# Three-stage Fourier and MLP kernel on one core: the odd outputs' two products of the second batch made one piece, and another order of the operations

## The chip, the core and the metric

The kernel runs on one core of one Trainium2 chip. The metric is the device time of one execution in microseconds (us). A core has engines that run side by side: TensorE (PE: matrix products; its weight loads are PEld), VectorE (DVE), ScalarE (ACT), GpSimd (POOL) and SyncE (SP), which here issues the transfers. Each engine works through its own instructions in the order in which the program gives them to it, and waits where an instruction needs what another engine, or a transfer, has not yet delivered.

## The reference

The input x has two batches of 3008 tokens with 256 values each. A Fourier transform along the tokens and one along the values are taken and the real part kept; the 6016 tokens that result go through two MLPs.

```python
X = np.fft.fft(x, axis=1)                    # x: (2, 3008, 256)
X = np.fft.fft(X, axis=2)
t = X.real.astype(np.float32).reshape(6016, 256)
h = t @ moe_w_in                             # (256, 2048)
r = np.maximum(h, 0.0)
t = (r * r) @ moe_w_out                      # (2048, 256)
h = t @ moe2_w_in
return (h * (1.0 / (1.0 + np.exp(-1.702 * h)))) @ moe2_w_out
```

## The kernel before

**Numbers in two halves.** The MLPs multiply in a rounded float32 format. So that the result keeps its precision, each operand is split into a rounded high part and a low part that holds the rest, and a product is made of three: high by high, high by low, low by high. The high part is a cast (on ScalarE, L1087), the low part a subtraction (`sub`, L182: `gl`, `eo`, `w`), which runs on VectorE or GpSimd. The weights come as pairs of 32-bit words and are put together by a run of small elementwise operations on ScalarE and VectorE (L294 to L324), named after the weight piece: `i0` to `i3` and `u0` to `u3` for the first MLP's two weights, `j` and `v` for those of the second.

**Stage 1** (until about 441 us) is everything up to the end of the first MLP. x is folded by symmetries (operations `f0` to `f5`, TensorE at L557 and L568; sums on VectorE at L489 to L520; copies out of PSUM on ScalarE at L281 and L595). Then the transform along the tokens is done as products with cosines and sines: for each batch b even outputs in two pieces (`e{b}0`, `e{b}1`, L693) and the odd outputs (`o{b}`). For the odd ones there are two products, `o{b}E0` (with `zc`) and `o{b}E1` (with `zs`), each of 16 matmuls at L652 into two PSUM banks; `o{b}c0`, `c1` copy one bank to SBUF, `o{b}s0`, `s1` (VectorE, L757 and L758) add and subtract the other, and the operations on `o{b}2` and `o{b}3` split the results, the last ones (`N`, at L768 in one case) making the value-axis part that only TensorE can turn around.

The 16 matmuls are emitted by `halves()` (L644). It multiplies parts with all 128 rows and parts with 64 rows, and its argument `turned` says which come first; by default the 64-row parts are last. The row count matters to the trace below: a product of 128 rows and one of 64 rows follow each other less tightly than two of the same kind.

**The first MLP** lies in the same stage, in 96 steps: six blocks of 512 tokens (one of 480, one of 484) by 16 slices of 128 hidden values, in the order `TURNS`. Step n has these operations:

- `Fn`: six matmuls (L791 to L793, three each for two banks, `psa`): the slice of h.
- `Pn`: VectorE adds a term of one row to the first bank (L1070), and the second bank to that and from that (L1072, L1073), which are the two halves of h. After L1070 the first bank is free, after L1073 the second.
- `Rn`: relu and square, on ScalarE in two halves (L1081, L1082) or on VectorE (L1079).
- `Hn` and `Gn`: the high part on ScalarE (L1087), the low part on GpSimd or VectorE (L182, `gl`).
- `Bn`: twelve matmuls with w_out (L806) into `psb`: eight of `gh` and four of `gl`.

**Stage 2** (441 to 937 us) is the second MLP, six blocks of eight units, TensorE at L1126 and L1147.

**What sets the order.** A string `ORDER` names every operation of stage 1 once, and the program emits them in that order; so it fixes each engine's queue. `HOME` names the engine of an operation where it isn't the usual one (A ScalarE, G GpSimd, V VectorE). `RINGS` says for six kinds of buffer which of them each use takes: `a0` and `a1` are the PSUM banks (two each) that `Fn`, the odd products and `o13N` write, `gh`, `gl`, `h` and `p` are buffers of the steps. All transfers go through SyncE's queue, in the order of the operations ending in `D`.

Of the kernel before, what the change touches and what calls it, by code (L numbers as in the profile page):

```python
# [40 lines left out]
f0D f0Db dfD f0a0 f0s0 f0p f0a1 df f0s1 f0m f1D f0mb f0pb f1s0 i0D f1a0 nD i0A f0E f1m f0Eb f1p i0L f2D ny f1u u0D nm
f0O f0Ob f0e1 c00D f1E nA f2s0 f1O nL f0e0 u0A f1e0 f2a0 f2m f2p c01D f2u f2E f1o c02D nC se i0C u0C f2O i0O f2e1 f0o
f2e0 i0S e00N nO i0P u0L i1D i0N f1e1 nS e00n f2o i0M u0S e00E u0O e00m e00c i0H e01E e01c e00s e01s i1L e01N c03D e00h
f0g f1g u0P e01n e00l i1O f2g e01h i1A i0l o0E0 o0c0 e01hb e01m i1C e01l
F0 nP i1S
F1 u0H P0 R0 o0s0 o0E1 H0 e01lb P1 u0l i1P o0c1 o0s1 G0 R1 o02h o02l o02hb f3D
F2 o02lb
F3 P2 B0 i1M o02N u1D P3
F4 H1 G1 o02n P4
F5 R2 R3 H2  # L50
F6 B1 i1N i1H R4 H3 u1L P5 u1A
F7 G2 i1l H4 B2 G3 G4 R5 P6 u1O H5
F8 P7 P8 u1C G5 B3 o03hb R6
F9 i2D i2A i2C u1S R7 X3.1 u1P i2S H6 G6 X3.0
F10 B4 H7 u1H u2D i2L B5 u1l P9 P10 R8 B6 G7 H8 i2O
F11 P11 R9
F12 G8 B7 u2L H9 R10 i3D i2P R11 H10 P12 G9 H11 u2O i2M B8 i2N i2H u2A
F13 G10 R12 G11 B9
F14 P13 u2C B10 i2l H12 G12 R13 P14
F15 i3A P15 B11 H13 G13 X11.0 X11.1  # L60
F16 i3C R14 B12 i3L H14
F17 R15 u2S H15 P16 P17
F18 u2P R16 G14 B13 o03h u2H R17 P18 i3S i3O
F19 H16 P19
F20 i3P G15 u2l B14 H17 G16 P20 R18 G17 H18 u3D i3N i3M u3L B15 R19 B16 H19 u3A
F21 G18 R20 H20
F22 u3O B17 P21 c10D P22 i3H G19 B18 G20 Y19 i3l
F23 R21 B19 H21 R22
F24 P23 G21 R23 H22 X19.0 X19.1 P24 R24 u3C
F25 H23 P25 R25 B20 o03l f3s0 H24 o03lb u3S  # L70
F26 G22 P26 B21 u3P G23
F27
F28 P27 R26 j0D B22 u3H B23
F29 P28 G24 o03N P29 R27 u3l f3a0 H25 f3m H26 H27 f4D G25 B24
F30 o03n G26 R28
F31 G27 f3p H28 f3v P30 R29 B25 Y27 G28 B26 B27 f4s0 f4a0 H29 P31 G29
F32 R30 H30 X27.0 X27.1 R31
F33 B28 c11D f3u P32 G30 P33
F34 H31 B29 f3w P34 R32 f4p f3E H32 f3O f3e0 R33 B30 G31 Y31 f4m
F35 B31 R34 f4u H33 G32 f3o P35  # L80
F36 G33 f5D H34 f3e1
F37 G34 X31.0 X31.1 R35 B32 P36 f5a0
F38 f5s0 f5m f4v R36 B33 P37 H35 P38
F39 f5p G35 B34 f4w H36
F40 P39 R37 f4O f5u P40 B35 G36 R38 v0D
F41 H37 f4o f4E R39 B36 H38 f5v P41 f4e0 f5w f4e1
F42 G37 R40 G38 f5E P42 f5e1 B37 f5e0 f5O H39 f5o =x e10E H40 e10n e10m G39 e10c
F43 e10s R41 e10h
F44 f5g B38 H41 R42 P43 H42 P44 e10l G40
F45 B39 P45 e11E e11n R43 G41 e11c e11m R44 R45 G42 e11s  # L90
F46 e11h c12D e11hb B40 e11l H43
F47 j0L P46 B41
F48 P47 H44 e11lb G43 f4g
F49 P48 c13D j0A j0C B42 R46 H45 j0S f3g B43
F50 j0O G44 H46 P49 R47 G45 R48
F51 P50 G46 B44 B45 H47
F52 B46 H48 R49 G47 R50 P51 G48 j0P B47 P52 H49 G49 H50 X47.0
F53
F54 X47.1 j01 B48 R51 P53 R52 H51 G50 P54 G51 j02 R53
F55 P55 H52 B49 G52 j03  # L100
F56
F57 P56 P57 R54 B50 j04 H53
F58 B51 j0H1 H54 G53 j0H0
# [1 line left out]
F60 B53 o1c1 o1s1 o12h j1D o12hb o12lb G56 o12l B54 o12N P60 o12n H57 H58 o13h
F61 R59 B55 G57 H59
F62 B56 P61 o13l G58 v0A R60 P62
F63
F64 G59 R61 H60 v0L =c B57 P63 R62 G60
F65 H61 R63 P64 v0O R64 P65 B58 v0C B59 v0S B60 R65  # L110
F66 v0P H62 G61 v1D P66 v0H H63
F67 G62 v0l P67 H64 o13N j1A B61 H65 tk o13n R66 R67 G63 G64
F68 B62
F69 G65 P68 P69 H66 R68 j1C R69 B63
F70 G66 X63.0 X63.1
F71 j1S j1L B64 H67 H68 B65 P70 R70 P71 G67 H69
# [18 lines left out]
F90 P89 H85 G85 H86 B84 G86 yaH
F91 ybH0 P90 R88 R89 H87 R90 ybl0 H88 P91 B85 B86 R91
F92 G87 P92 G88
F93 H89 R92 yal P93 H90
F94 y2 B87 B88 H91 G89 y3 G90 G91 R93
F95 ybH1 P94 B89 B90 P95 H92 G92 ybl1 H93 R94 B91 G93 H94 R95 G94 H95 B92 G95  # L140
# [1242 lines left out]
```

## Time and profile before

| | |
|---|---|
| median of 3 runs | 939.01 us (938.97 to 939.48) |
| the profiled execution | 939.21 us, span of its instructions 937.0 us |
| granted TensorE clock | 1.00 of full speed in every stretch (the 2.4 GHz level) |
| TensorE busy | 930.3 us of the span (99%) |
| busy until 40 us, 40 to 441 us, 441 to 937 us | 38.00, 400.44, 491.83 us |

The span runs from the first to the last instruction on the core; the execution's own time is 2.2 us longer. In a row of the timeline stand the start, the time from the start of the first to the end of the last of the x instructions put together, the engine, the line, the operation, what it writes and reads, and in square brackets how long the engine sat idle before it and what ended that. Matmuls are pipelined: one begins before the last has ended, so the distance from start to start is what one costs TensorE.

### The profile page before, as it was taken

Reading aid. Unit: us, or ns where it says so; the run is one execution under the profiler, and the core shown is the slowest. Engines: PE = TensorE matmul, PEld = TensorE weight load, DVE = VectorE, ACT = ScalarE, POOL = GpSimd, SP = SyncE. Lnnn points to the kernel's source line nnn. Section 1 sums busy time; section 2 is a strip of 40 time slices with the busy share of each in tenths; the row PEclk is TensorE's granted clock in tenths of the full one; section 3 lists DMA queues with packets and bytes.
Section 4 is the critical chain, followed back from the end, with each engine's and each line's share of the span. In section 5 each row is a group of like instructions: output and inputs, shape, how many; then the busy total and the mean of one; then the engine's idle time right before and its main releaser. Section 6 shows DMA issues by size and latency. Waiting matters only on the chain.

```text
span 937.0 us, 10882 instructions
## 1 busy us (share of the span) xinstructions
PE 930.3 (99%) x4274; PEld 777.5 (83%) x4274; DVE 693.1 (74%) x807; ACT 574.8 (61%) x620; POOL 252.6 (27%) x139
## 2 busy tenths in 40 slices
PE   9999999999999999999999999999999999999998
PEld 9688888888878788888888888888888888888886
DVE  7999999988976889978888665665675576466453
ACT  4798987557667775686766544544454455455443
POOL 0668486602333646353123200020030011000000
PEclk9999999999999999999999999999999999999999
DMA  8521333600200120200320100110010011000001
GB/s 316 200 74 62 116 135 127 239 3 24 68 21 0 45 91 1 75 16 7 126 91 1 59 29 1 45 46 1 1 66 22 1 43 46 0 1 39 7 1 43
DMA packets 12915, 53.53 MB, mean 57 GB/s; under 512 B 1344, under 2 KB 4544, under 8 KB 9664
## 3 DMA queue, kind: packets, MB, share of 16 engines
q1 hardware_dynamic: 12864, 52.84, 15.5%
q8 instruction: 33, 0.54, 0.2%
q14 instruction: 18, 0.15, 0.0%
HBM read 37.36 MB, written 15.48 MB: 56 GB/s over the span
## 4 chain that ended last, share of the span: by engine, by line
PE 91%; DVE 5%; ACT 2%; DMA 1%; issue 0%; SPq 0%; DVEq 0%; ACTq 0%
PE psb L1147 27%; PE psb L806 25%; PE psc L1126 22%; PE psa L791 4%; PE psa L792 4%; PE psa L793 4%; PE psa L652 1%; PE psb L652 1%; DMA xt<-in_x 1%; PE psa L568 1%; DVE gl L182 1%; PE psa L693 1%; DVE ue L312 0%; ACT zc L595 0%; DVE t L489 0%
## 5 line engine op out<-in xcount | busy, mean ns | idle before, releaser
L806 PE MATMUL psb<-gh,w 128*128 128x512 f32 (+2 forms) x768 | 215.3, 387 | 0.0
L182 POOL TENSOR_TENSOR gl<-h,gh 128x1024 fp32r<-128x1024 f32 (+2 forms) x56 | 141.3, 2532 | 134.6 <-PE psb L806 58.3
L806 PEld LDWEIGHTS psb<-gh,w 128*128 128x128 f32 x768 | 143.7, 188 | 27.8 <-ACT h L1082 0.5
L1147 PE MATMUL psb<-gh,w 128*128 128x512 f32 (+2 forms) x576 | 163.9, 386 | 0.0
L1218 DVE TENSOR_TENSOR g<-u,psc 128x1024 f32<-128x1024 f32 (+2 forms) x48 | 57.6, 1200 | 115.8 <-PE psc L1126 115.8
L1220 ACT ACTIVATE g<-g 128x1536 f32<-128x1536 f32 (+2 forms) x48 | 70.4, 1467 | 95.5 <-DVE g L1218 95.5
L1147 PEld LDWEIGHTS psb<-gh,w 128*128 128x128 f32 x576 | 108.1, 188 | 20.8
L1087 ACT CAST gh<-h 128x1024 fp32r<-128x1024 f32 (+2 forms) x96 | 97.8, 1029 | 38.6 <-PE psb L806 30.8
L806 PE MATMUL psb<-gl,w 128*128 128x512 f32 (+2 forms) x384 | 117.2, 386 | 0.0
L182 DVE TENSOR_TENSOR gl<-g,gh 128x2048 fp32r<-128x2048 f32 (+3 forms) x50 | 110.4, 2212 | 0.4 <-ACT gh L1195 0.4
L1081 ACT ACTIVATE h<-h 128x1024 f32<-128x1024 f32 (+2 forms) x79 | 81.8, 1036 | 18.1 <-DVE h L1073 18.1
L1195 ACT CAST gh<-g 128x2048 fp32r<-128x2048 f32 (+3 forms) x50 | 90.4, 1813 | 0.1
L911 POOL TENSOR_TENSOR ue<-raw 128x512 f32<-128x512 f32 (+2 forms) x12 | 22.1, 1863 | 249.7 <-DMA raw<-ydram 243.3
L1147 PE MATMUL psb<-gl,w 128*128 128x512 f32 (+2 forms) x288 | 87.9, 386 | 0.1
L1082 ACT ACTIVATE h<-h 128x1024 f32<-128x1024 f32 (+2 forms) x79 | 82.4, 1043 | 2.5
L806 PEld LDWEIGHTS psb<-gl,w 128*128 128x128 f32 x384 | 72.1, 188 | 14.0
L1070 DVE SCALAR_TENSOR_TENSOR p<-n,w1n_t,psa 128x512 f32<-128x512 f32 (+2 forms) x96 | 70.0, 729 | 12.0 <-PE psa L793 11.8
L1217 ACT ACTIVATE g<-psc 128x512 f32<-128x512 f32 (+2 forms) x48 | 28.4, 592 | 76.2 <-PE psc L1126 76.2
L791 PE MATMUL psa<-eo,w 128*128 128x512 f32 (+2 forms) x192 | 74.7, 389 | 0.0
L793 PE MATMUL psa<-eo,w 128*128 128x512 f32 (+2 forms) x192 | 74.1, 386 | 0.0
L792 PE MATMUL psa<-eo,w 128*128 128x512 f32 (+2 forms) x192 | 74.1, 386 | 0.0
L1072 DVE TENSOR_TENSOR h<-p,psa 128x512 f32<-128x512 f32 (+2 forms) x96 | 65.0, 677 | 12.2 <-DVE p L1070 1.0
(186 smaller groups left out, 1528.1 us busy)
## 6 DMA issues: line engine op xcount, KB each, us to landing
ydram<-o SPq DMA_DIRECT2D x14, 512.0 KB, 2.8
xt<-in_x SPq DMA_DIRECT2D x5, 1024.0 KB, 5.9
cst<-in_dfts SPq DMA_DIRECT2D x8, 576.0 KB, 7.3
raw<-in_w1i SPq DMA_DIRECT2D x4, 1024.0 KB, 5.6
raw<-in_w1o SPq DMA_DIRECT2D x4, 1024.0 KB, 7.8
raw<-in_w2i SPq DMA_DIRECT2D x4, 1024.0 KB, 5.2
raw<-in_w2o SPq DMA_DIRECT2D x4, 1024.0 KB, 4.9
raw<-ydram SPq DMA_DIRECT2D x4, 1024.0 KB, 4.7
```

What stands on the lines that cost most here:

```text
L182: eng.tensor_tensor(out=o, in0=a, in1=f32(b), op=ALU.subtract)
L791: T.matmul(o, lhsT=w[:, 0, fs], rhs=t[:, par, 0, 0:wd], start=True, stop=False)
L792: T.matmul(o, lhsT=w[:, 0, fs], rhs=t[:, par, 1, 0:wd], start=False, stop=False)
L793: T.matmul(o, lhsT=w[:, 1, fs], rhs=t[:, par, 0, 0:wd], start=False, stop=True)
L806: T.matmul(acc[j][ec][:, s, 0:wd], lhsT=w[:, hl, e0:e0 + P], rhs=(gh, gl)[gi][:, s, 0:wd], start=(first and hl == 0 and gi == 0), stop=(la ...
L1081: A.activation(out=hv, in_=hv, func=AF.Relu)
L1082: A.activation(out=hv, in_=hv, func=AF.Square)
L1087: A.copy(st["gh"][:, :, 0:wd], st["h"][:, :, 0:wd])
L1126: T.matmul(bank, lhsT=w[:, hl, slot * P:(slot + 1) * P], rhs=x[:, yl, 0:wd], start=(first and hl == 0 and yl == 0), stop=(hl == 1), skip_g ...
L1147: T.matmul(o[:, s, 0:wd] if j < BLKS - 1 or ec == 0 else o[s][:, 0:wd], lhsT=weights[1, 1, f // 4][:, hl, e0:e0 + P], rhs=g[:, 2 * i + s, ...
L1195: A.copy(gh[:, at], gs[u - 1][:, at])
L1220: A.activation(out=g[:, 1:4], in_=g[:, 1:4], func=AF.Gelu_apprx_sigmoid)
```

## The change

Three things change.

1. `halves` is called with `turned=True` for the second of the two odd products, in both batches: it takes its 64-row parts first.
2. In the second batch the two products `o1E0` and `o1E1` become one operation `o1E`, so that nothing can stand between their matmuls: the 64-row parts that end the first product are followed by the 64-row parts that begin the second. In the first batch they stay `o0E0` and `o0E1`.
3. `ORDER` is another one throughout stage 1, and `HOME` and three of the `RINGS` (`a0`, `a1`, `h`) go with it. In the first 96 steps VectorE has 29 of the low parts G where it had 40 (GpSimd 67 where it had 56), and 15 of the R where it had 17; six low parts of the second MLP's w_in move from GpSimd to VectorE (GpSimd 2 where it had 8).

Line numbers of the changed kernel are higher by 1 up to about L740 and by 7 behind it (the odd products at L653, `Fn` at L798 to L800, `Bn` at L813, `o13N` at L775).

```diff
--- before.py
+++ after.py
...
-F59 j0l0 P58 G54 R55 P59 R56 o1E0 j0l1 o1E1 H55 B52 o1c0 G55 R57 R58 H56 o1s0
...
+F59 B52 H55 P59 o1E j0l0 H56 R58 G55 o1c0 o1s0
...
-    "a0": "0101010101010101010101010101010101010101010101010101010101010101010101010101010101010101010101010101"
+    "a0": "0101010101010101010101010101010101010101010101010101010010101010101010101010101010110101010101010101"
-    "a1": "0100101010101010101010101010101010101010110101010101010101010101010101010101010101010101010101010101"
+    "a1": "0100101010101010101010101010101010101010101010101010101011010101010101010101010101010101010101010101"
...
@@ -738,14 +739,20 @@
             w = make().rearrange("p a b -> p (a b)")
             return w[:, 0:wd], *(w[:, i * wd:(i + 2) * wd].rearrange("p (r k) -> p r k", r=2) for i in (1, 3))
 
+        both = []
         for par in range(2):
-            @op(f"{name}E{par}")
-            def _(par=par):
+            def sums(par=par):
                 c0, c1 = cst[b, 2][:, :, 0:wd], cst[b, 3][:, :, 0:wd]
                 pe = held[par] = ps_b() if f"{name}E{par}" in IN_B else ps_a()
                 z = (zc[b], zs[b])[par]
                 halves(pe[:, 0, 0:wd], pe[:, 1, 0:wd],
-                       [(z[:, :, 2 + par, 0:P], c0), (z[:, :, 3 - par, 0:P], c1)])
+                       [(z[:, :, 2 + par, 0:P], c0), (z[:, :, 3 - par, 0:P], c1)], turned=par == 1)
+
+            if b:
+                both.append(sums)
+                ops[f"{name}E"] = lambda: [f() for f in both]
+            else:
+                ops[f"{name}E{par}"] = sums
 
             @op(f"{name}c{par}")
             def _(par=par):
```

The order itself is best seen on the engines. **TensorE at the odd products of the second batch** (about 270 to 283 us in the trace of before). Before, the operations are B51, F58, F59, o1E0, o1E1, B52, F60; the rows show the second half of that, from F59 on:

```order
L791 MATMUL psa<-eo,w 128x512
L792 MATMUL psa<-eo,w 128x512
L793 MATMUL psa<-eo,w 128x512
L652 MATMUL psa<-cst,zc 128x376 x8
L652 MATMUL psa<-cst,zs 128x376 x8
L806 MATMUL psb<-gh,w 128x512 x2
L806 MATMUL psb<-gl,w 128x512 x2
L806 MATMUL psb<-gh,w 128x512 x4
```

After, they are F59, B52, o1E, F60, B53:

```order
L813 MATMUL psb<-gh,w 128x512 x2
L813 MATMUL psb<-gl,w 128x512 x2
L813 MATMUL psb<-gh,w 128x512 x4
L813 MATMUL psb<-gl,w 128x512 x2
L813 MATMUL psb<-gh,w 128x512 x2
L653 MATMUL psa<-cst,zc 128x376 x8
L653 MATMUL psa<-cst,zs 128x376 x8
L798 MATMUL psa<-eo,w 128x512
L799 MATMUL psa<-eo,w 128x512
L800 MATMUL psa<-eo,w 128x512
```

B52 has moved from behind the two products to ahead of them, and what follows them now is F60, whose banks come from the same two rings as theirs. (The order counts eight matmuls for an odd product, the trace sixteen records.)

**TensorE at `o13N`** (about 316 us before; sel_t is the small matrix by which it multiplies). Before, F66 and F67 stand right ahead of it:

```order
L791 MATMUL psa<-eo,w 128x512
L792 MATMUL psa<-eo,w 128x512
L793 MATMUL psa<-eo,w 128x512
L768 MATMUL psa<-eo,sel_t 128x376 x2
L806 MATMUL psb<-gh,w 128x512 x2
L806 MATMUL psb<-gl,w 128x512 x2
```

After, F64, F65 and B57 do, and F66 comes behind it:

```order
L813 MATMUL psb<-gh,w 128x512 x4
L813 MATMUL psb<-gl,w 128x512 x2
L813 MATMUL psb<-gh,w 128x512 x2
L775 MATMUL psa<-eo,sel_t 128x376 x2
L798 MATMUL psa<-eo,w 128x512
L799 MATMUL psa<-eo,w 128x512
```

Between `o13N` and the last F there are now the twelve matmuls of a B.

**ScalarE in the first 22 us.** The two-row products of x leave PSUM through `zc` and `zs` (L595 and L281; L596 and L282 after), which the folds of the later parts wait for; L294 and L300 (L295 and L301 after) widen weights: ue<-raw is the piece `i0` the first time, `u0` the second time. Before:

```order
L294 ACTIVATE ue_132<-raw_128 128x1024
L300 ACTIVATE ue_132<-raw_128 128x1024
L440 ACTIVATE nyq_106<-nyq_106 128x24
L595 ACTIVATE zc_200<-psa_163,nyq_106 128x65 x4
L294 ACTIVATE w1n_t_105<-w1n_raw_101 128x16
L300 ACTIVATE w1n_t_105<-w1n_raw_101 128x16
L595 ACTIVATE zc_200<-psa_134,nyq_106 128x65 x4
L294 ACTIVATE ue_234<-raw_184 128x1024
L595 ACTIVATE zc_200<-psa_207,nyq_106 128x65 x4
L281 COPY zs_258<-psb_220 128x512
```

After:

```order
L301 ACTIVATE w1n_t_105<-w1n_raw_101 128x16
L441 ACTIVATE nyq_106<-nyq_106 128x24
L295 ACTIVATE w1n_t_105<-w1n_raw_101 128x16
L282 COPY zs_197<-psb_162 128x512
L295 ACTIVATE ue_216<-raw_190 128x1024
L301 ACTIVATE ue_216<-raw_190 128x1024
L596 ACTIVATE zc_222<-psa_126,nyq_106 128x65 x4
L301 ACTIVATE ue_227<-raw_193 128x1024
L596 ACTIVATE zc_222<-psa_155,nyq_106 128x65 x4
L596 ACTIVATE zc_222<-psa_234,nyq_106 128x65 x4
```

The widening of u0 stands between the first and the second copy of zc, where before the second copy of zc stood ahead of it and one more behind it.

## Rows read from the trace of the kernel before

**Rows 1.** The page: busy time of each engine over the span.
```profile
PE 930.3 (99%) x4274; PEld 777.5 (83%) x4274; DVE 693.1 (74%) x807; ACT 574.8 (61%) x620; POOL 252.6 (27%) x139
```

**Rows 2.** TensorE's waits: line waited at, releaser, us in total, times, longest.
```profile
PE psa L768 <- DVE p L1070: 0.6, 1, 0.6
PE psb L652 <- ACT ue L300: 0.5, 1, 0.5
```

**Rows 3.** Timeline of TensorE, even outputs and first odd product of batch 0.
```profile
24.16 0.49 PE L693 MATMUL psa<-cst,zc 64*128 64x189 f32 x4
24.48 0.49 PE L693 MATMUL psa<-cst,zs 64*128 64x189 f32 x4
24.89 0.91 PE L693 MATMUL psa<-cst,zc 128*128 128x189 f32 x4
25.64 1.19 PE L693 MATMUL psa<-cst,zs 128*128 128x189 f32 x4
26.66 0.80 PE L693 MATMUL psb<-cst,zc 128*128 128x188 f32 x4
27.30 0.80 PE L693 MATMUL psb<-cst,zs 128*128 128x188 f32 x4
28.03 0.59 PE L693 MATMUL psb<-cst,zc 64*128 64x188 f32 x4
28.45 0.48 PE L693 MATMUL psb<-cst,zs 64*128 64x188 f32 x4
30.59 4.23 PE L652 MATMUL psb<-cst,zc 128*128 128x376 f32 x16 [0.50 <-ACT ue L300]
```

**Rows 4.** Timeline of TensorE, the two odd products of batch 1.
```profile
272.35 4.15 PE L652 MATMUL psa<-cst,zc 128*128 128x376 f32 x16
276.43 4.26 PE L652 MATMUL psa<-cst,zs 128*128 128x376 f32 x16
280.62 0.73 PE L806 MATMUL psb<-gh,w 128*128 128x512 f32 x2
```

**Rows 5.** Timeline of TensorE, VectorE and GpSimd around the wait at L768.
```profile
316.16 0.39 PE L792 MATMUL psa<-eo,w 128*128 128x512 f32 x1
316.39 0.39 PE L793 MATMUL psa<-eo,w 128*128 128x512 f32 x1
317.33 0.61 PE L768 MATMUL psa<-eo,sel_t 128*128 128x376 f32 x2 [0.56 <-DVE p L1070]
...
311.46 2.89 DVE L312 TENSOR_SCALAR ue<-ue 128x1024 uint32<-128x1024 uint32 x1
...
316.54 0.73 DVE L1070 SCALAR_TENSOR_TENSOR p<-n,w1n_t,psa 128x512 f32<-128x512 f32 x1
...
311.40 2.40 POOL L182 TENSOR_TENSOR gl<-h,gh 128x1024 fp32r<-128x1024 f32 x1 [0.52 <-PE psb L806]
```

**Rows 6.** Timeline of ScalarE, 18 to 20 us.
```profile
18.62 1.16 ACT L294 ACTIVATE ue<-raw 128x1024 f32<-128x1024 f32 x1 [2.15 <-DMA raw<-in_w1o]
```

**Rows 7.** Instructions of L312 and L182: count, ns min/median/max, first and last start.
```profile
L312 DVE TENSOR_SCALAR ue<-ue x14: 678/690/2901, 21.6 to 476.5; 128x1024 uint32<-128x1024 uint32 x14
...
L182 POOL TENSOR_TENSOR gl<-h,gh x56: 2211/2414/3468, 41.4 to 433.1; 128x1024 fp32r<-128x1024 f32 x43, 128x968 fp32r<-128x968 f32 x8, 128x960 fp32r<-128x960 f32 x5
...
L182 DVE TENSOR_TENSOR gl<-h,gh x40: 1147/1213/2141, 68.5 to 440.9; 128x1024 fp32r<-128x1024 f32 x21, 128x960 fp32r<-128x960 f32 x11, 128x968 fp32r<-128x968 f32 x8
```

**Rows 8.** Timeline of VectorE, GpSimd and TensorE, first steps of the MLP.
```profile
37.96 0.54 DVE L757 TENSOR_TENSOR ue<-ue,psb 128x376 f32<-128x376 f32 x1
...
38.88 0.74 DVE L1070 SCALAR_TENSOR_TENSOR p<-n,w1n_t,psa 128x512 f32<-128x512 f32 x1
...
40.92 1.22 DVE L324 CUSTOM_DVE_ANT_0 ue<-ue 128x2048 uint16<-128x2048 uint16 x1
...
41.38 3.04 POOL L182 TENSOR_TENSOR gl<-h,gh 128x1024 fp32r<-128x1024 f32 x1 [2.07 <-ACT gh L1087]
...
45.02 0.61 PE L806 MATMUL psb<-gl,w 128*128 128x512 f32 x2
```

More of the change, by code (lines that the diff above doesn't have):

```diff
@@ L37 @@
 WARM = {0: 24, 2: 2}
-HOME = {**dict.fromkeys("""u0L j0L v0L v1L X3.1 X11.1 X63.1 X79.1""".split(), "A"), **dict.fromkeys("""f3s0 f4s0 f5s0 i0l u0l i3l u3l u1l e01l e01lb o02l o02lb i1M i3M o03l e10l e11l o12lb o12l o13l y0 y1 ybl1""".split(), "G"), **dict.fromkeys("""i1l o0c1 o02n R5 R7 G6 G10 i2l R13 G16 G17 G18 R20 G24 G26 G27 R33 G36 G37 G38 G39 G40 e11n G41 G43 G44 G45 G46 G47 R50 j01 R51 G52 R54 j04 G53 G54 o1c0 G56 o12n G57 G58 G60 R65 R68 R69 G69 G70 G71 j14 R74 R76 R77 G75 G76 R79 G78 G81 G83 G85 R90 G87 G90 G93 R95 G94 G95""".split(), "V")}
+HOME = {**dict.fromkeys("""u0L v0L v1L X3.1 X11.1 X63.1 X79.1""".split(), "A"), **dict.fromkeys("""f3s0 f4s0 f5s0 i0l u0l u3l u1l e01l e01lb o02lb o02l i1M i2M i3M o03l e10l e11l o12l o13l y0 y1 y3""".split(), "G"), **dict.fromkeys("""i3l i1l j0L o0c1 o02n R5 R7 G6 G10 G11 i3L G13 R19 G19 G20 G27 G28 G32 G37 G38 f5o G39 R43 R44 e11n e11c G42 R49 G47 G49 j0l0 G55 o1c1 R59 R61 G58 o12n o13n G61 G64 R67 G65 G66 j1L R68 G69 j13 R77 R78 G77 j1l1 j1l0 R83 G80 G81 R91 G92 G93 R95 G94 G95""".split(), "V")}
@@ L39 @@
 IN_B = ('f0O', 'f1O', 'f2O', 'e00N', 'e01E', 'e01N', 'o0E0', 'o0E1')
 ORDER = """
[L41 to L103, printed above, removed]
@@ L104 @@
-F59 j0l0 P58 G54 R55 P59 R56 o1E0 j0l1 o1E1 H55 B52 o1c0 G55 R57 R58 H56 o1s0
[L105 to L116, printed above, removed]
@@ L135 @@
[L135 to L140, printed above, removed]
+f0D f0Db f0a0 dfD f0s0 nD f0p f1D f0s1 f0a1 f0m df f0mb f0E f0pb f1a0 se f0O f1s0 f1p f1m f0Ob f2D ny f1u f2s0 nL i0D nm
+u0D nA f2a0 f0o f2m f2p f0Eb f1O i0A nC f2u i0C i0L f0e0 u0L nO f0e1 f1E f1e0 f2E i0O i0S f1o c02D i0P f2O f2e0 c01D
+c00D i1D u0O f2e1 f2o u0A e00N e00E i0M i0N nS f1e1 e01E u0C nP e00n e00c i0H u0S e00s i1L e01c c03D e00m f1g e00h e01s
@@ new lines @@
+i1A e00l f0g u0P e01N i0l e01n e01m i1C u1D e01hb o0E0 e01h i1O e01l o0c0 i1S
+F0 o0s0 P0 u0H
+F1 u0l f2g P1 o0E1 e01lb i1P o0c1
+F2 R0 o0s1
+F3 i2D H0 P2 R1 G0 o02hb o02h H1 B0 P3 R2 u1A o02lb o02l o02N i1N i1M o02n
+F4 P4 H2 i1H
+F5 R3 R4 H3 P5 G1 H4 G2 G3 B1
+F6 u1C
+F7 B2 R5 u1S i1l G4 P6 u1L
+F8 B3 u1O f3D P7 u2D H5 i2L i2A G5 X3.0 R6 P8 i2C
+F9 u1P
+F10 i2S X3.1 R7 P9 H6 u1H R8 B4 H7 G6 u2L H8 u1l P10 i2O c11D B5 R9
+F11 P11 R10 H9 G7 B6
+F12 B7 i2P c12D G8 P12 R11 H10 i3D H11 G9 i2M
+F13 P13 B8 G10 R12 i2N G11 u2A i2H i2l H12 B9
@@ new lines @@
+F14
+F15 B10 u2C G12 R13 i3A P14 B11 P15 o03h
+F16 u2O H13 X11.0
+F17 X11.1 u3D i3C R14 u2S i3L i3S G13 u2P H14 P16 B12 u2H B13
+F18 P17 i3O R15 H15 G14 R16
+F19 u2l P18 H16 G15 R17 P19 B14 H17
+F20 R18
+F21 G16 B15 R19 G17 P20 i3P i3M i3N P21 H18 R20
+F22 B16 H19 P22 o03hb G18 G19 H20 i3H i3l f3s0 B17 R21
+F23 R22 B18 G20 H21 Y19 P23 G21 B19 X19.0
+F24 H22 X19.1 P24
+F25 u3A u3L P25 B20
+F26 R23 f3a0 P26 o03l
+F27 B21 R24 H23 G22 u3C P27 H24 R25 o03lb u3O j0D u3S H25 G23 f3m G24 R26 u3P
+F28 B22 u3H P28 H26 B23 R27 u3l
@@ new lines @@
+F29
+F30 R28 f4D P29 B24 G25 G26 f3p H27
+F31 P30 H28 B25 G27 o03N B26 R29 H29 R30 f4a0 G28 B27 P31 f3v
+F32 o03n G29 H30 Y27 R31 H31 X27.0
+F33 G30 X27.1 B28 P32 P33 f4s0 f4m R32 R33 f4p
+F34 B29 P34 H32 G31 G32 f3u
+F35 R34 B30 f3w Y31 P35 H33 c10D f3O G33 f3o f3E f3e1 B31 f4v X31.0 R35 f3e0 X31.1
+F36 P36
+F37 H34 B32
+F38 P37 v0D G34 H35 f4u
+F39 P38 f4w B33
+F40 R36 G35 R37 P39 H36 P40 f5D G36 f4O
+F41 f5s0 B34 f4o P41 f5a0 f5p f5m R38
+F42 H37 f4E H38 B35 G37 P42 B36 f5u R39 f5v f5w R40 H39 f4e1 f4e0 f5O f5E f5e0 R41 G38 B37 f5e1 f5o e10E G39 e10n =x
@@ new lines @@
+e10m e10c
+F43 e10s
+F44 P43 B38 H40
+F45 B39 e10h P44 G40 f4g H41 c13D P45 R42 R43 R44 e11E e10l e11n G41 e11c H42 R45 G42 B40 f5g e11s H43 G43 e11h H44 e11m
+F46 P46 e11l e11hb
+F47 e11lb j0A R46 B41 P47 H45
+F48
+F49 G44 P48 B42 R47
+F50 R48 P49 H46 j0L B43 G45 P50
+F51 G46 j0C B44 H47
+F52 B45 P51 H48 R49 R50 H49 R51 G47 B46 P52 G48 B47
+F53 j0S G49 H50 X47.0 R52 j0O X47.1
+F54 j0P B48 G50 P53 H51
+F55 j1D j01 B49 j02 R53 H52 P54 P55
+F56 R54 G51 j03
+F57 G52 B50 j04 R55 f3g P56
+F58 H53 j0H1 P57 B51 G53 j0H0 R56 P58 R57 j0l1 H54 G54
@@ new lines @@
+F59 B52 H55 P59 o1E j0l0 H56 R58 G55 o1c0 o1s0
+F60 o1c1 o1s1 B53 G56
+F61 o12h o12hb R59 H57 P60 B54 o12lb P61 R60 G57 o12l
+F62 P62 B55 R61 H58 o12N o13h G58 o13l H59
+F63 B56 v0A P63 o12n v0L G59
+F64 H60
+F65 R62 R63 B57 P64 H61 v0O o13N G60 P65
+F66 B58 H62 B59 o13n
+F67 v0C G61 tk R64 v0S P66 B60 H63 B61
+F68 H64 R65 G62 v0P G63 P67 v0H
+F69 B62 G64 H65 R66 v0l H66 R67 P68 P69 G65 B63 G66 j1L v1D X63.0 j1A R68
+F70 X63.1 H67
+F71 j1C j1S P70 R69 B64
+F72 G67 B65 P71 P72 j1O j1P
+F73 H68 R70 R71 H69 =c R72
@@ new lines @@
+F74 G68 B66 P73 j11 G69 B67
+F75 H70 P74 H71
+F76 G70 B68 P75
+F77 B69 G71 P76 B70 R73 j12 H72 H73
+F78 G72 R74 j13 B71 G73 R75 H74 P77 R76 G74
+F79 R77 j14 P78 P79
+F80 H75 B72 G75 R78 H76 j1H1
+F81 B73 P80 yD G76 R79
+F82 H77 B74 R80 P81 H78 R81
+F83 G77 j1H0 B75 j1l1 P82 G78 B76
+F84 H79 G79 H80 P83 P84 j1l0 R82 B77 R83 v1A v1C G80 H81 B78 v1L G81 B79 X79.0
+F85 X79.1 v1S H82 R84 B80 G82 v1O P85
+F86 P86 H83 G83
+F87 P87 H84 R85 v1P B81
+F88 jlD R86 G84
+F89 B82 v1H P88 P89 H85
+F90 R87 G85 B83 v1l P90 H86
@@ L141 @@
+F91 R88 H87 B84 G86
+F92 G87 P91 P92
+F93 R89 y0 B85 y2 R90 B86 R91 H88
+F94 H89 H90 B87 G88 y1 G89 R92 ybH1 G90 P93 P94
+F95 B88 H91 y3 P95 yaH B89 ybl1 R93 G91 H92 R94 yal B90 H93 G92 G93 H94 R95 ybH0 B91 G94 H95 ybl0 B92 G95
 """
 RINGS = {
-    "a0": "0101010101010101010101010101010101010101010101010101010101010101010101010101010101010101010101010101"
+    "a0": "0101010101010101010101010101010101010101010101010101010010101010101010101010101010110101010101010101"
           "0101010101010101",
-    "a1": "0100101010101010101010101010101010101010110101010101010101010101010101010101010101010101010101010101"
+    "a1": "0100101010101010101010101010101010101010101010101010101011010101010101010101010101010101010101010101"
@@ L148 @@
     "gl": "012012012012012012012012012012012012012012012012012012012012012012012012012012012012012012012012",
-    "h": "0123402134021343042130421423014230123401234013420134201342013420134202013420134201342013134201342013"
-          "4201343420134201",
+    "h": "0123402134021341402314020231402314031240312402341024130241302413024131302413024130241302024130241302"
+          "4130202413024130",
     "p": "0101010101010101010101010101010101010101010101010101010101010101010101010101010101010101010101010101"
```

18 lines of the change are left out of this document (removed).

## The prediction, made before the changed kernel had run

> **What bounds the kernel now.** I read the page's busy times first: TensorE is busy for 930.3 of 937.0 us [rows 1]. So nothing that another engine gains or loses counts unless TensorE waits for it or stops waiting for it, and no other engine is close behind it: VectorE has 693.1 us. The second view is the list of TensorE's waits. Past the start there are two in stage 1 that this change can touch: one at L768 (`o13N`) for VectorE's L1070, and one of about 0.5 us at L652 (`o0E0`) [rows 2]. The third view is the timeline of TensorE, in which I look at the distance from one start to the next, because there a cost shows that is no wait: the switch between products of 128 and of 64 rows. Stage 2 (491.83 us of TensorE in 496) is not changed, so what the change does it does before 441 us, and the matmuls it emits are the same ones. All that can move is: switches, waits that go, waits that come.
>
> **The fused product.** The even outputs of batch 0 show what a switch costs, as four like pieces stand there with and without one [rows 3]. Four matmuls of 64 rows take 0.32 us (24.16 to 24.48) when the next are of 64 rows too, 0.41 when 128 rows follow (24.48 to 24.89), and 0.42 when they are the first after 128 rows (28.03 to 28.45). Four of 128 rows take 0.64 (26.66 to 27.30) between their own kind, 0.73 when 64 rows follow (27.30 to 28.03) and 0.75 when they are the first after 64 rows (24.89 to 25.64). So going into 64 rows costs 0.09 + 0.10 and going out 0.09 + 0.11: 0.39 for a pair. `o1E0` and `o1E1` now each go in and out; their starts are 4.08 and 4.19 us apart from the next [rows 4], 8.27 together. In `o1E` the first ends and the second begins in 64 rows, so one pair is saved: **-0.39**, and `o1E` should take 7.88. Bounds: nothing saved (if the switch of the constants costs as much) and -0.39. In batch 0 `F` matmuls stand between the two products, all of 128 rows, so `o0E1` goes in and out once whether turned or not: 0.
>
> What is moved here: B52 goes ahead of the products, and F60 comes right behind them. It writes banks of the rings that the products take, so it waits for the copy `o1c0` and the sum `o1s0` of the first product. These have the 3.8 us of the second product; the sum is 0.92 (L757 to the next L1070 [rows 8]) and the copy, of one bank of 376, is no longer than that. Cost 0; if ScalarE or VectorE comes 2 us late to them, it shows as a wait at L798.
>
> **`o13N`.** TensorE starts it 0.94 us after the last matmul of F67, where matmuls of 512 start 0.23 apart (316.16 to 316.39) [rows 5]. So 0.71 us is lost, for a bank that P66 frees. P66's L1070 began at 316.54 because a weight operation on VectorE (L312, begun at 311.46) took 2.89 us, against a median of 0.69 [rows 5, 7]. It began 0.06 us after a GpSimd low part (311.40, 2.40 long, thus over at 313.80) and ended 0.55 us after it. In the new order `o13N` needs the bank of P64, and the twelve matmuls of B57 (12 by 0.23, 2.7 us) are between F65 and `o13N`; P64 is then over some 3 us earlier. **-0.71**; bounds -0.71 and 0, the latter if the stretch has another late P. The next to be late is F66 behind it, whose first bank P65's L1070 frees. Counted from F64's first matmul, with F64 and F65 of 1.36 us each: P64 runs on VectorE from 1.36 for 2.04 (L1070 to the operation behind the P, 38.88 to 40.92 [rows 8]), then a weight operation like that L324 (`v0O`, 1.22), then P65's L1070 (0.74), over at 5.4. F66 begins at 1.36 + 1.36 + 2.7 + 0.46 (`o13N`'s two) = 5.9: slack 0.5, less some 0.2 for semaphores, an estimate. So no wait, but little room.
>
> **The start.** ScalarE's order decides here. In before it waited 2.15 us for the weight piece u0 and began its L294 at 18.62, which took 1.16 [rows 6]. After, i0's two widenings come ahead and u0's comes between two copies that TensorE waits for in the folds of f2. With the landing as it was, the copy of `zc` behind it ends near 20.5 (18.62 + 1.16 + some 0.8) and e00N begins some 0.2 us later than it did. Against that, the sums f2o come earlier, and the wait in the even outputs goes: four matmuls of zs took 1.02 us (25.64 to 26.66) where such take 0.64 [rows 3], 0.38 lost. The end of this stretch is `o0E0`, which waits about 0.5 us for the end of the even outputs' sums [rows 2, 3]; those depend on the last even product, which comes out at about its old time. So `o0E0` starts near 30.6, and F0 some 4.1 us behind it, near 34.7, as before: **0**, bounds -0.9 (the 0.38 and the 0.50 both go) and +0.6 (the 0.2 and an u0 landing 0.4 us later). Past that point each us by which u0 lands later is one us lost.
>
> **The first steps.** `o0s0` (0.92) now stands ahead of P0 on VectorE, where it stood behind it. R0, H0 and G0 move by as much. G0 ran on GpSimd from 41.38 to 44.42, and its use in B0 is at 45.02 [rows 8]: 0.60 of slack against 0.92. If G0 takes its 3.04 again, the wait is 0.32; if it takes the median 2.41 [rows 7], none. I take **+0.1**, bounds 0 and +0.32.
>
> **The low parts.** Eleven G go from VectorE (1.21 each) to GpSimd (2.41 each) [rows 7]: VectorE has 13.3 us less of them, and GpSimd 26.5 more. Their longer time is covered by the lead between a step's P and its B: counted in TensorE's matmuls between a step's F and its B, at 0.23 each, the new order gives 1.9 us more on the mean, and a moved G wants 1.2 more. Cost 0; if the cover is gone, 1.2 us for a step at most. There is a price beside it: a GpSimd low part holds off VectorE operations, as L312 above; that is the main rival.
>
> The Trainium skill says of this (page "SBUF — State Buffer", section "SBUF: two separate sides") that VectorE and GpSimd share a pair of ports as an exclusive lock which one of them holds for its whole instruction. By that rule the 26.5 us more on GpSimd are 26.5 us in which such VectorE operations cannot start, for 13.3 us saved, and it speaks against this part of the change. The trace agrees in kind: L312's 2.89 us ended 0.55 us after the GpSimd operation did.
>
> **The sum.** -0.39 - 0.71 + 0 + 0.1 = -1.0. The profiled execution took 939.21 us, so 938.2; it lies 0.2 above the median of the runs, 939.01, and against that the forecast is **938.0 us**.
>
> **The rivals.**
> 1. *A VectorE operation is held off where slack is small (the other side).* From P4 to P9, about 50 to 62 us, where VectorE has a P, an R or a weight operation at every moment, I count in the way shown for P65 only about 0.25 us of slack for P6 and P8 (the banks of F8 and F10), and before F66 the 0.3 above. One operation held as L312 was costs 2.90 - 0.69 = 2.2, less the slack 1.9 us at TensorE [rows 7]. For it: more work on GpSimd. Against: VectorE has 13 us less, and elsewhere the count gives 2 us and more. One such event gives 938.0 + 1.9 = 939.9, with the gains it decides the sign as soon as TensorE loses more than 1.0 us; slower by over 0.2% needs 2.9 us, two of them.
> 2. *The start is later.* u0's widening ahead of a copy that TensorE waits for: +0.6 gives 938.6, and if u0 lands 2 us later, 940.
> 3. *The fusing or the move of `o13N` does nothing* (another wait of the same size comes in its place): 938.4 or 938.7; both, 939.1.
> 4. *The start wait goes too:* -0.9 more, 937.1.
>
> **How the numbers follow.** No change can be told from the measurement below about 0.2%, 1.88 us: 937.13 to 940.89. The forecast with small misses (937.4 to 938.7) has 0.52. Gains eaten by new waits (rivals 1 once, 2, or 3: 938.7 to 940.9) have 0.28. Slower than 940.9 (two held operations, or one with a late start) has 0.13. Under 937.1 (rival 4) has 0.07. So faster 0.07, same 0.80, slower 0.13. The range that leaves out no more than 2 in 10 is 937.0 to 940.2: it takes all terms at their best end but for some tenths (-0.39 - 0.71 - 0.9 gives 937.0) and leaves out two held operations.
>
> **What the new profile would show.** If the fusing is right, `o1E` takes 7.9 us from its first start to F60's, not 8.27, and there is no wait at L798 behind it. If the second term is right, L775 stands in no wait, and F66 in none either. If the start is right, F0 begins between 34.6 and 34.9 and the wait at L653 is still there. B0's first matmul with the low part should wait 0.3 us or less. GpSimd should be busy for about 275 us and VectorE for about 682. I am wrong if TensorE's list of waits has a new entry above 1 us that VectorE or ScalarE releases, above all at L798 to L800 between 45 and 65 us or near 316, with a VectorE operation of over 2 us before it.

## The result, and the profile after

The changed kernel takes 945.27 us (median of 4 runs, 943.56 to 945.94), before 939.10 (4 runs); the ratio is 1.0062 with a 95% interval of 1.005 to 1.0074. It is 6.2 us slower, where 1.0 less was forecast. The profiled execution took 945.16, its span is 943.4. The page's busy times after the change answer to [rows 1]:

```profile
PE 932.6 (99%) x4274; PEld 778.6 (83%) x4274; DVE 688.7 (73%) x804; ACT 574.1 (61%) x618; POOL 263.8 (28%) x146
```

The list of TensorE's waits answers to [rows 2]:

```profile
PE psa L798 <- DVE p L1077: 3.4, 2, 3.0
PE psa L798 <- DVE n L282: 1.3, 1, 1.3
...
PE psb L653 <- ACT eo L665: 0.4, 1, 0.4
PE psa L798 <- DVE h L1080: 0.4, 1, 0.4
```

The wait at `o13N` is gone, and three new lines stand at L798, the matmuls of `F`, all released by VectorE (of the two waits in the first line, 3.0 and 0.4, the second comes later, at F41). The timeline of TensorE shows where:

```profile
48.29 0.39 PE L800 MATMUL psa<-eo,w 128*128 128x512 f32 x1
49.96 0.50 PE L798 MATMUL psa<-eo,w 128*128 128x512 f32 x1 [1.28 <-DVE n L282]
...
59.15 0.61 PE L813 MATMUL psb<-gh,w 128*128 128x512 f32 x2
62.76 0.47 PE L798 MATMUL psa<-eo,w 128*128 128x512 f32 x1 [3.00 <-DVE p L1077]
...
64.09 0.50 PE L798 MATMUL psa<-eo,w 128*128 128x512 f32 x1 [0.39 <-DVE h L1080]
...
65.01 1.05 PE L813 MATMUL psb<-gh,w 128*128 128x512 f32 x2
65.86 1.05 PE L813 MATMUL psb<-gl,w 128*128 128x512 f32 x2
66.72 1.75 PE L813 MATMUL psb<-gh,w 128*128 128x512 f32 x4
```

These are F5 and the two halves of F8. And what follows F8 is slow without a wait: two matmuls of B3 stand 0.85 us from the next two (65.01 to 65.86), where two take 0.46 elsewhere. The view by windows (TensorE's busy time first, the granted clock behind POOL's) says why:

```profile
59.50:64.66 5.16, 1.77 (x8) 0.97 (x7) 5.03 (x5) 2.18 (x2) 4.71 (x2) 1.00 0.00 0
64.66:68.10 3.44, 3.44 (x10) 2.66 (x9) 3.24 (x5) 0.24 (x1) 0.00 (x0) 0.51 0.53 150
68.10:75.00 6.90, 6.90 (x32) 5.71 (x31) 6.63 (x10) 6.84 (x8) 1.20 (x1) 1.00 0.73 266
```

TensorE was idle for 3.4 of the 5.2 us before, and then ran for 3.4 us at the lower level, 1.2 GHz. What VectorE and GpSimd did meanwhile answers to [rows 5]:

```profile
46.41 0.68 DVE L1080 TENSOR_TENSOR h<-p,psa 128x512 f32<-128x512 f32 x1
47.00 2.38 DVE L363 SCALAR_TENSOR_TENSOR ue<-ue,misc 128x512 f32<-128x512 f32 x1
49.30 0.60 DVE L282 COPY n<-psa 128x270 f32<-128x270 f32 x2
...
54.59 1.22 DVE L1086 SCALAR_TENSOR_TENSOR h<-h 128x1024 f32<-128x1024 f32 x1
55.73 2.93 DVE L313 TENSOR_SCALAR ue<-ue 128x1024 uint32<-128x1024 uint32 x1
58.58 3.38 DVE L183 TENSOR_TENSOR w<-ue,w 128x1024 fp32r<-128x1024 f32 x1
61.88 0.73 DVE L1077 SCALAR_TENSOR_TENSOR p<-n,w1n_t,psa 128x512 f32<-128x512 f32 x1
...
46.43 2.40 POOL L183 TENSOR_TENSOR gl<-h,gh 128x1024 fp32r<-128x1024 f32 x1
...
55.69 2.41 POOL L183 TENSOR_TENSOR gl<-h,gh 128x1024 fp32r<-128x1024 f32 x1 [4.03 <-PE psa L800]
...
58.06 2.82 POOL L183 TENSOR_TENSOR gl<-h,gh 128x1024 fp32r<-128x1024 f32 x1
...
60.84 3.37 POOL L183 TENSOR_TENSOR gl<-h,gh 128x1024 fp32r<-128x1024 f32 x1
```

Three operations of VectorE begin while a GpSimd low part runs and last 2.38, 2.93 and 3.38 us; the same forms take 0.75, 0.69 and 1.2 where GpSimd is idle. The first stands ahead of the copy `o02n`, which frees F5's bank. The other two stand ahead of P6, which frees F8's.

Where the 6.4 us of the span come from is read from the starts of like matmuls in both timelines. F0 begins 0.6 earlier; F5's last matmul is 1.0 later, F8's last 4.9 later, F9 6.5 later (64.66 to 68 at the lower level is in that); it stays at 6.5 up to F38. The wait at F5 with its restart is thus 1.6, those at F8 3.9, the clock 1.6: 7.1 in the first ten steps. Behind them come 0.7 at F41 and 0.4 in small waits, the fused product gives back 0.4 and `o13N` 0.8. -0.6 + 7.1 + 1.1 - 1.2 = 6.4.

The rows ahead of F41 show the same there, though no run tests it alone. A sum of the folds (L521, 0.69 us otherwise) is held by a low part, G35, which was on GpSimd before too, and VectorE runs without a pause from it to the L1077 for which F41 waits:

```profile
189.65 2.54 DVE L521 TENSOR_TENSOR xt<-xt 128x512 f32<-128x512 f32 x1
...
189.36 2.27 POOL L183 TENSOR_TENSOR gl<-h,gh 128x960 fp32r<-128x960 f32 x1 [2.44 <-ACT h L1088]
...
197.45 0.49 PE L798 MATMUL psa<-eo,w 128*128 128x480 f32 x1 [0.40 <-DVE p L1077]
```

Held operations as such are not new. Counted as VectorE operations of stage 1 that last over 0.5 us longer than the shortest of their form in the two traces, there are 19 before and 19 after. But the first of before begins at 101 us and only one of them, the L312 of [rows 5], shows as a wait of TensorE; after, three begin before 62 us.

### The profile page after: what moved, and what is told of

Read it like the earlier page. It is cut to its first block, busy times and chain, and to the rows that moved or that the text cites. A ratio compares the mean times of both kernels' runs of the same rounds, so it can differ in the third digit from the quotient of the medians.

```text
span 943.4 us, 10897 instructions
## 1 busy us (share of the span) xinstructions
PE 932.6 (99%) x4274; PEld 778.6 (83%) x4274; DVE 688.7 (73%) x804; ACT 574.1 (61%) x618; POOL 263.8 (28%) x146
## 4 chain that ended last, share of the span: by engine, by line
PE 95%; DVE 3%; DMA 1%; ACT 0%; issue 0%; SPq 0%; DVEq 0%
PE psb L1154 27%; PE psb L813 27%; PE psc L1133 24%; PE psa L798 4%; PE psa L800 4%; PE psa L799 4%; PE psa L653 1%; PE psb L653 1%; PE psa L569 1%; DMA xt<-in_x 1%; PE psa L694 1%; DVE p L1077 0%; PE psb L569 0%; DVE h L1080 0%; DVE h L1079 0%; DVE w L183 0%
## 5 line engine op out<-in xcount | busy, mean ns | idle before, releaser
L813 PE MATMUL psb<-gh,w 128*128 128x512 f32 (+2 forms) x768 | 216.5, 388 | 0.0
L183 POOL TENSOR_TENSOR gl<-h,gh 128x1024 fp32r<-128x1024 f32 (+2 forms) x67 | 165.4, 2474 | 158.2 <-PE psb L813 64.6
L813 PEld LDWEIGHTS psb<-gh,w 128*128 128x128 f32 x768 | 144.6, 189 | 27.7
L813 PE MATMUL psb<-gl,w 128*128 128x512 f32 (+2 forms) x384 | 117.5, 387 | 0.0
L183 DVE TENSOR_TENSOR gl<-g,gh 128x2048 fp32r<-128x2048 f32 (+3 forms) x50 | 109.5, 2193 | 0.4 <-ACT gh L1202 0.4
L1088 ACT ACTIVATE h<-h 128x1024 f32<-128x1024 f32 (+2 forms) x81 | 84.0, 1038 | 14.4 <-DVE h L1080 12.4
L1089 ACT ACTIVATE h<-h 128x1024 f32<-128x1024 f32 (+2 forms) x81 | 84.7, 1045 | 2.6
L813 PEld LDWEIGHTS psb<-gl,w 128*128 128x128 f32 x384 | 72.4, 189 | 14.1
L798 PE MATMUL psa<-eo,w 128*128 128x512 f32 (+2 forms) x192 | 75.7, 394 | 5.1 <-DVE p L1077 3.4
L1077 DVE SCALAR_TENSOR_TENSOR p<-n,w1n_t,psa 128x512 f32<-128x512 f32 (+2 forms) x96 | 70.2, 731 | 9.6 <-PE psa L800 9.6
L800 PE MATMUL psa<-eo,w 128*128 128x512 f32 (+2 forms) x192 | 74.3, 387 | 0.0
```

The source lines that it names most:

```text
L183: eng.tensor_tensor(out=o, in0=a, in1=f32(b), op=ALU.subtract)
L798: T.matmul(o, lhsT=w[:, 0, fs], rhs=t[:, par, 0, 0:wd], start=True, stop=False)
L800: T.matmul(o, lhsT=w[:, 1, fs], rhs=t[:, par, 0, 0:wd], start=False, stop=True)
L813: T.matmul(acc[j][ec][:, s, 0:wd], lhsT=w[:, hl, e0:e0 + P], rhs=(gh, gl)[gi][:, s, 0:wd], start=(first and hl == 0 and gi == 0), stop=(la ...
L1088: A.activation(out=hv, in_=hv, func=AF.Relu)
L1089: A.activation(out=hv, in_=hv, func=AF.Square)
```

## The experiments

The theory is that these three held operations, with the clock's fall behind them, are the loss, and that it is the places of three weight operations in the new order, not the number of low parts on GpSimd, that put them there. The rivals: VectorE simply has too much to do there; or GpSimd's longer hours cost time everywhere.

**The fused product alone**, in the order of before:

```diff
-F59 j0l0 P58 G54 R55 P59 R56 o1E0 j0l1 o1E1 H55 B52 o1c0 G55 R57 R58 H56 o1s0
+F59 j0l0 P58 G54 R55 P59 R56 o1E j0l1 H55 B52 o1c0 G55 R57 R58 H56 o1s0
```

> The order of before, with the one edit that o1E0 and o1E1 are one operation o1E whose second product takes its 64-row parts first. If a pair of row switches is what the fusing saves: 0.39 us less (about 938.7 against 939.1), and in the trace 7.88 us from the first start of o1E to the next matmul behind it, where it was 8.27. If the change of the constants costs as much as the switch: 8.27 and 939.1.

938.73 us (11 runs) against 939.15, ratio 0.9996 (0.9987 to 1.0005): the size of the forecast, though this ratio alone can't be told from 1. The trace can tell it; its two products and what follows answer to [rows 4]:

```profile
272.25 4.15 PE L652 MATMUL psa<-cst,zc 128*128 128x376 f32 x16
276.24 4.15 PE L652 MATMUL psa<-cst,zs 64*128 64x376 f32 x16
279.94 0.92 PE L812 MATMUL psb<-gh,w 128*128 128x512 f32 x2
280.70 0.62 PE L812 MATMUL psb<-gl,w 128*128 128x512 f32 x2
```

The second product now begins with its 64 rows (64x376 in the row). From its first start to the last row 8.45 us pass. Before, the row that answers to the last one is this:

```profile
281.19 0.63 PE L806 MATMUL psb<-gl,w 128*128 128x512 f32 x2
```

From 272.35 [rows 4] to it 8.84 us pass: 0.39 saved. (The next matmul's start comes earlier, at 7.69, and its own distance is 0.30 longer than 0.46, so the sum is to be taken past it.)

**The first wait**: in the changed kernel `o02n` goes ahead of the held operation.

```diff
-... o02lb o02l o02N i1N i1M o02n
+... o02lb o02l o02N o02n i1N i1M
```

> The changed kernel, with VectorE's copy o02n put ahead of the two weight operations i1N and i1M that stand before it. Theory (F4 waits 1.28 us because the copy that frees its bank stands behind L363, which a GpSimd low part holds for 2.38 us instead of 0.75): the wait at F4 goes, 1.4 us less, so about 943.8 where all that follows stays as it was. Rival (F4 waits for another user of the bank, or the order of VectorE alone is too long there): the wait stays, 945.2.

942.64 us (4 runs; 1.0036, 1.0023 to 1.005). The bank that waited is F5's, not F4's as the expectation says; its wait is gone. The gain of 2.6 is larger than 1.4, as all that follows is shifted: P6 is held once, not twice (i1l, 3.43 us, begun 0.1 after a low part), F8 waits 1.8 and 0.4, and in the profiled execution (941.75, the fastest of the four) the clock stays at its upper level.

**Without three low parts.** Here the result isn't the reference's: the low parts of steps 3 to 5 are replaced by copies on ScalarE.

```diff
-            sub(on(f"G{i}", "G"), gl[:, :, 0:wd], st["h"][:, :, 0:wd], gh[:, :, 0:wd])
+            if i in (3, 4, 5):
+                A.copy(gl[:, :, 0:wd], st["h"][:, :, 0:wd])
+            else:
+                sub(on(f"G{i}", "G"), gl[:, :, 0:wd], st["h"][:, :, 0:wd], gh[:, :, 0:wd])
```

> The changed kernel, with the low parts of steps 3, 4 and 5 left out: copies of h on ScalarE stand in their places and in their waits, so GpSimd does nothing between about 52 and 64 us. Theory (GpSimd's three low parts hold off VectorE's L313 and the subtraction i1l, 2.93 and 3.38 us long, and so P6): both take 0.7 and 1.2 us, the waits of 3.0 and 0.4 us of F8 and F9 go, the granted clock stays at its upper level behind them, and about 5.5 us are saved: 939.7. Rival (the new order gives VectorE too much between P5 and P6, whoever else works): the wait at F8 stays above 2 us, and the time above 943.

940.02 us (10 runs; 1.001, 1.0001 to 1.0019), 0.3 beside the theory's 939.7. (The waits that the expectation puts at F8 and F9 are those of the two halves of F8.) The timeline, of VectorE with the same operations in the same order as after the change, and F8's first matmul:

```profile
55.09 1.22 DVE L1086 SCALAR_TENSOR_TENSOR h<-h 128x1024 f32<-128x1024 f32 x1
56.22 0.69 DVE L313 TENSOR_SCALAR ue<-ue 128x1024 uint32<-128x1024 uint32 x1
56.82 1.22 DVE L183 TENSOR_TENSOR w<-ue,w 128x1024 fp32r<-128x1024 f32 x1
57.96 0.74 DVE L1077 SCALAR_TENSOR_TENSOR p<-n,w1n_t,psa 128x512 f32<-128x512 f32 x1
...
60.15 0.39 PE L798 MATMUL psa<-eo,w 128*128 128x512 f32 x1
```

P6's L1077 is over at 58.70, F8 begins at 60.15 without a wait: 1.45 us of slack, behind a wait at F5 that both runs have. The two holds cost 2.93 + 3.38 - 0.69 - 1.22 = 4.40; less that slack it is 2.95, and 3.00 was the wait. So VectorE's queue is not too long by itself. The wait at F5, left as it was, is still 1.3.

**Both moves**: u1S (L313) goes behind P6 as well.

```diff
-F7 B2 R5 u1S i1l G4 P6 u1L
+F7 B2 R5 i1l G4 P6 u1S u1L
```

> The changed kernel with two moves on VectorE alone: o02n ahead of i1N, as in the run before, and the weight operation u1S (L313) from ahead of i1l to behind P6. Theory (in the run with the first move alone the waits left in the first ten steps, 1.8 and 0.4 us at F8 and F9 with their restarts, come from i1l, held for 3.43 us because L313 ahead of it let a GpSimd low part begin 0.1 us before it): i1l now begins before that low part, takes 1.2 to 1.4 us, both waits go, and 942.6 becomes about 940.0. Rival (the held place only moves, to u1S or the operation behind it, and P7 comes late in the place of P6): a wait of 1 to 2 us at F9 or F10, 941 to 942.

941.20 us (11 runs; 1.0022, 1.0012 to 1.0031): the rival's figure. i1l is no longer held, but the hold has moved on:

```profile
55.53 1.22 DVE L183 TENSOR_TENSOR w<-ue,w 128x1024 fp32r<-128x1024 f32 x1
56.67 0.74 DVE L1077 SCALAR_TENSOR_TENSOR p<-n,w1n_t,psa 128x512 f32<-128x512 f32 x1
...
59.51 3.42 DVE L319 SCALAR_TENSOR_TENSOR ue<-raw,ue 128x1024 uint32<-128x1024 uint32 x1
62.85 0.73 DVE L1077 SCALAR_TENSOR_TENSOR p<-n,w1n_t,psa 128x512 f32<-128x512 f32 x1
...
56.03 9.13 POOL L183 TENSOR_TENSOR gl<-h,gh 128x1024 fp32r<-128x1024 f32 x3 [3.96 <-ACT gh L1094]
```

GpSimd has three low parts with no pause between them, and L319 ahead of P7 meets the second. P7 is late, and F9 and F10 wait (1.0, 0.5 and 0.4).

**One of the three on VectorE**, on top of both moves:

```diff
-... """i3l i1l j0L o0c1 ...
+... """i3l i1l G4 j0L o0c1 ...
```

> The changed kernel with the two moves of before (o02n ahead of i1N, u1S behind P6) and, in addition, the low part of step 4 on VectorE (1.2 us, behind i1l) and not on GpSimd, so that GpSimd has two low parts there and not three in a row. Theory (what holds L319 for 3.42 us is the low part that GpSimd begins with no pause behind the one before): GpSimd is idle when L319 comes, which takes 1.2 to 1.4 us, the waits behind it (1.4 with its restart, 0.8 and 0.7) go although VectorE has 1.2 us more to do, and the time is 938.8 to 939.5. Rival (VectorE has too much there in any case): 941.2 or more.

943.08 us (4 runs; 1.0041, 1.0026 to 1.0056). The expectation was wrong. The moved low part itself is held by the one before it, which stayed on GpSimd:

```profile
56.89 3.15 DVE L183 TENSOR_TENSOR gl<-h,gh 128x1024 fp32r<-128x1024 f32 x1 [0.19 <-issue]
59.96 0.73 DVE L1077 SCALAR_TENSOR_TENSOR p<-n,w1n_t,psa 128x512 f32<-128x512 f32 x1
...
55.97 6.30 POOL L183 TENSOR_TENSOR gl<-h,gh 128x1024 fp32r<-128x1024 f32 x2 [3.95 <-ACT gh L1094]
```

The windows behind it show what that does to TensorE (columns as above):

```profile
58.40:60.84 2.44, 0.11 (x1) 0.03 (x1) 2.34 (x3) 2.43 (x3) 2.44 (x2) 0.99 0.00 0
60.84:64.00 3.16, 3.16 (x7) 2.30 (x8) 3.16 (x5) 0.00 (x0) 1.43 (x1) 0.50 0.02 5
```

L319 is free now (1.21 us), as expected, but P6 is late by the new hold: its L1077 ends at 60.69, F8 begins at 60.84 after 2.3 us of waiting, and 3.2 us at the lower clock follow. (The list of waits names ScalarE's L295 there, which ended at 60.83; but the 0.15 us from L1077's end to F8 is the same as in the changed kernel, 62.61 to 62.76.) The work that left GpSimd gained nothing here, as it landed on VectorE while another GpSimd operation ran.

**A hold put into the kernel before**: one weight operation of 0.75 us is moved.

```diff
-F4 H1 G1 o02n P4
+F4 H1 G1 i1N o02n P4
...
-F6 B1 i1N i1H R4 H3 u1L P5 u1A
+F6 B1 i1H R4 H3 u1L P5 u1A
```

> The kernel before, with one operation of VectorE moved: the weight operation i1N (L362, 0.75 us) from behind P4 to right ahead of the copy o02n, as the changed order has it. Theory (i1N then begins while GpSimd's low part of 47.26 to 49.68 runs and is held until it ends, and the copy that frees F5's bank is as late): L362 takes 2 to 2.4 us, TensorE waits about 1.2 us at F5, and the time is 1.2 to 1.5 us longer, 940.5. Rival (there is room for such an operation in the old order): the same as before within 0.3.

940.87 us (11 runs) against 939.18, ratio 1.0018 (1.0009 to 1.0027): 1.7 longer, a little more than the 1.2 to 1.5 expected. The timeline has the held operation, the copy behind it and the low part that holds it:

```profile
47.50 2.55 DVE L362 SCALAR_TENSOR_TENSOR ue<-ue,misc 128x512 f32<-128x512 f32 x1
49.97 0.60 DVE L281 COPY n<-psa 128x270 f32<-128x270 f32 x2
...
47.10 2.40 POOL L182 TENSOR_TENSOR gl<-h,gh 128x1024 fp32r<-128x1024 f32 x1
```

and the list of TensorE's waits what F5 makes of it:

```profile
PE psa L791 <- DVE n L281: 1.5, 1, 1.5
```

The home of every low part is that of before here. A place in the order is enough.

**The order of before for the first ten steps, the changed one from F10 on.** The first splice put a P on a buffer whose low part was not yet out:

> The order and the engines of before up to F10, of the changed kernel from there on. Theory (all of the loss lies in the first ten steps, where three VectorE operations are held off; behind that the changed order loses about 1.1 in small waits and wins 0.4 by the fusing and 0.8 at o13N): 939.0. Rival (GpSimd's longer hours cost time everywhere): 941 or more, with waits at L798 spread over 70 to 440 us.

947.98 us (4 runs; 1.0095, 1.008 to 1.0111), with a wait of 6.7 us at F11, at the seam, that neither kernel has. So it says nothing on the question; it was run again with another choice of buffers.

> Once more the order of before up to F10 and that of the changed kernel from there on, now with the five buffers h taken in rotation. (The list of these buffers of the changed kernel put a P at the seam on a buffer whose low part was not yet out: 6.7 us of waiting that neither kernel has.) Theory (behind the first ten steps the changed order is worth what before is, small waits of 1.1 against gains of 1.2): 939.0. Rival (more GpSimd work costs in the rest too): above 940 with waits beyond 75 us.

938.94 us (10 runs) against 939.18, ratio 0.9997 (0.9988 to 1.0007): the theory's 939.0. GpSimd has 67 low parts here, as in the changed kernel, and TensorE is busy for 400.43 of the 401 us from 40 to 441; what it waits for there is 0.2 us at F11, next to the seam, and 0.3 at F41.

**What was forecast as gain, alone**: the fused product and `o13N` behind B61, all else as before.

```diff
-F67 G62 v0l P67 H64 o13N j1A B61 H65 tk o13n R66 R67 G63 G64
+F67 G62 v0l P67 H64 B61 o13N j1A H65 tk o13n R66 R67 G63 G64
```

> The order of before with the fused o1E and with o13N moved from ahead of B61 to behind it. The first alone gave 0.42 less. If o13N's wait of 0.71 (with its restart some 0.8) goes as in the changed kernel: 1.1 to 1.2 less, 938.0. If another matmul waits in its place: 938.7.

937.96 us (11 runs) against 939.18, ratio 0.9987 (0.9978 to 0.9996). It beats both kernels. It is also 1.0 less than the spliced kernel's 938.94, which has the same two gains: so from F10 on the rest of the changed order is not quite free. In the spliced kernel's trace the wait at F11 costs 0.5 with its restart and the one at F41 0.6, with the same sum of the folds held for 2.47 us. TensorE's waits left are these three, all before 31 us:

```profile
PE psa L447 <- DVE still L267: 1.1, 1, 1.1
PE psa L568 <- DVE xt L520: 1.0, 1, 1.0
PE psb L652 <- ACT ue L300: 0.5, 1, 0.5
```

**The same with the changed kernel's order up to F0**:

> The fused o1E and the moved o13N in the order of before, with the changed kernel's order and engines up to F0. Theory (the changed start is worth nothing: F0 began at 34.16, 34.96, 34.64 and 34.49 with it, and at 34.75, 34.63, 34.60 and 34.57 without): 938.0, as without it. Rival (the profiled execution of the changed kernel shows its worth, 0.59): 937.4.

937.77 us (10 runs), ratio 0.9981 (0.9972 to 0.9991). 0.2 less than without, where the runs of either reach over 0.5 and more; its F0 begins at 34.76. The 34.16 of the changed kernel's profile is not seen again in any of the five other traces with that start (34.44 to 34.96).

## Why the prediction was wrong

- **The fused product** (-0.39): right. 0.39 in the trace, 0.42 in the medians; no wait behind `o1E`.
- **`o13N`** (-0.71): right. No wait there, none at F66, and together with the fusing 1.2 less in the runs.
- **The start** (0): right as a forecast; the changed kernel's profile gave 0.6 less, which the other traces with the same start don't repeat (34.44 to 34.96, around the 34.6 to 34.9 forecast).
- **The low parts** (0 for the eleven that move to GpSimd): nearly right from F10 on; with the changed order there, all 67 on GpSimd, 939.18 became 938.94, which is 1.0 above 937.96 for the old order with the same two gains. The 0.6 of that at F41 is read off behind a low part that did not change its engine. GpSimd and VectorE were forecast to be busy for 275 and 682 us and were for 263.8 and 688.7: the low parts on GpSimd grew by 24 us about as forecast, but the six of w_in, which go the other way, took 9.7 with them.
- **The first steps** (+0.1): wrong, and this is the step that failed. G0 took 2.42 and B0 didn't wait, as the lower bound had it. But the term looked at one moved operation only, `o0s0`, and it came to +7.1. What the runs showed in its place: i1N, now ahead of `o02n`, held for 2.38 (1.6 us at F5; put into the old order by itself, 1.7 us); u1S and i1l, now both ahead of P6, held for 2.93 and 3.38 (3.9 us at F8); and 1.6 us of the lower clock behind that wait.
- **The first rival** had the mechanism, the place (P6, F8) and the price of one hold (1.9 us), and was weighed too low, for two reasons. It counted the holds by chance, one within 0.28 and two within 0.13, with VectorE's 13 us less against it; but whether an operation is held is decided by the rows of the order. In these ten steps not one low part had changed its engine. What had changed was which weight operations stand behind R5 and ahead of a P, just when GpSimd gets its next low parts, and the order shows that. Second, it priced one hold at a time and without the clock. One hold at P6 costs about what it said: in the run with `o02n` first, i1l lost 2.2 and F8 waited 1.8, which leaves 0.4 of slack where 0.25 was counted. (The 1.45 of the run without the low parts stands behind the wait at F5, which makes TensorE late too.) Two in a row cost 3.9, with the lower clock behind them.
- **The clock** was not in the sum: before, it stood at 1.00 as long as TensorE worked, and no row there has TensorE idle for 3 us. Of the changed kernel's four runs the three with a mean clock of 0.997 or 0.998 took 945.16 to 945.94, the one with 1.000 took 943.56.

What stays open: a change of two places in the first ten steps was not enough to mend the changed order (941.20), and no version of its head that costs nothing was found other than the old one.
